# A fused attention and SwiGLU kernel: the halves of the partitions exchanged by token tiles instead of by heads, and one more group scored in 64-key blocks

## The chip, the cores and the metric

The kernel runs on one core of a Trainium2 chip. The core has TensorE (matmul; the profile calls it PE, and its weight loads PEld), VectorE (DVE), ScalarE (ACT), GpSimd (POOL) and SyncE (SP), each with its own queue of instructions worked off in order, and DMA engines that they share. Here POOL issues the loads that convert from float32 to bfloat16, and SP and ACT issue the stores and the transposing DMAs. The metric is the device time of one execution in microseconds (us), the median of several runs.

## The reference

Two parts follow each other: attention over a sliding window of 128 keys plus 4 sink keys at the start of the sequence, and a feed-forward block on its output.

```python
# q, k, v: (4 batches, 8 heads, 768 tokens, 64), float32; n_sink 4, window 128
scores = scale * np.matmul(q, k.transpose(0, 1, 3, 2))
keep = is_sink | ((rel >= 0) & (rel < window))        # rel = query - key
scores = np.where(keep, scores, -1e9)
a = np.exp(scores - max); a = a / (sum(a) + 1e-9)
attn = np.matmul(a, v)
# x: (3072 tokens, 512), the eight heads side by side
g = x @ w_gate                                         # 512 x 1536
out = (silu(g) * (x @ w_val)) @ w_out                  # 1536 x 512
```

## The kernel before

**Groups and tiles.** The 3072 tokens are cut into 12 groups of 256 queries, three for each batch: group g is part c = g % 3 of batch b = g // 3. Attention runs group by group. The feed-forward part runs over eight blocks of 256 or 512 tokens and is cut into units: a `gate` unit is two sets of matmuls of 512 columns in sum (gate, line 506 "pg"; value, line 506 "pv"), with a tanh on ACT (L526) and two products on DVE, `u` (L534) and `ht` (L536, L541 or L545); a `down` unit is the product with `w_out` (L591) and a store.

**The order is written by hand.** The function `weave` goes through a list of units; `slots` says which attention steps are put into which unit, between its gate matmuls and its value matmuls. All engines run their instructions in the order in which they are written. DVE work that is not urgent (masks, normalisations) is collected in a list `later` and put into DVE's queue by `flush`, at the end of a gate unit behind that unit's `u` and `ht`.

**Attention of one group.**
- `load_nat` fetches K and Q (L112, four DMAs from POOL's queue), `load_v` fetches V. Groups 2 and 3 are turned by TensorE (`step_TN`, L265), groups 4 and up by transposing DMAs on SP (`xbar`, L279).
- `step_S` computes scores transposed, keys on the partitions and queries along the columns; ACT takes the exponential out of PSUM (L321, L368) into the tile `e`; DVE multiplies the mask in (L326, L372). It is called twice for a group, for heads 0 to 3 and for heads 4 to 7 (`p2` = 0 and 1), each time for two pairs of heads.
- `step_K` computes the scores of the sink keys. `step_sinks` starts the output of all four PSUM tiles `pos[j, hh]` (j: first or second 128 queries; hh: heads 0 to 3 or 4 to 7) with the sinks' products (L403).
- `step_PV` adds the products with V (L441) for one (j, hh), and normalises (L449, L455, or L452 on ACT). The first `step_PV` of a group calls `step_sinks`.
- `step_X` turns the result for the feed-forward part.

**Two ways of scoring.** Groups with c = 0, and groups 1 and 2, use whole blocks of 128 keys: for a pair of heads and c > 0, three matmuls for each head of 128, 256 and 128 columns on half of the array (64 rows by 128 columns, a head in each half). That gives 512 columns of `e`, a quarter of them in blocks that the window does not reach. PV is two matmuls of 128 keys for each head and each j: 32 for the group.

The groups in the list `QG` (4, 5, 7, 8, 10 and 11) use `step_Sq`: key blocks of 64, on quarters of the array (64 rows by 64 columns). A block of 64 queries meets three blocks of 64 keys, so the four query blocks of a group have twelve such cells. They are laid into six slots of 64 columns with two halves of partitions, 384 columns of `e` for each head. Slots 0 and 1 hold two full halves of keys for j = 0, slots 4 and 5 for j = 1; so PV takes one full matmul of 128 keys for each head and j (16 in the group). Slots 2 and 3 hold the cells that are left, and these take quarter products: 32 matmuls of 64 keys and 64 queries, in `step_sinks` (L414), for all eight heads.

**Which half of the partitions.** A key block goes either to the lower 64 partitions or to the upper 64. In `step_Sq` this is `odd ^ p2`: heads 4 to 7 have the halves exchanged against heads 0 to 3. The mask tile `maskq` therefore has two versions, and the tile of V, `vms[b]` (six slots of 128 partitions for a batch), has a different token layout for heads 0 to 3 and heads 4 to 7; `load_vm` fills it with DMAs of four heads each, ten for c = 1 and six for c = 2 (L127).

**Where things stand in the queues.** POOL's queue begins with loads for groups 0 and 1 and gate weights 0 to 2, then `step_vsb(0)`, K and Q of group 2, gate weights 3, V of group 2 (two DMAs, L147), gate weights 4 and 5, the output weights, K, Q and V of group 3, two memsets, the sinks of the later batches on SP, and `build_maskq` (one memset L332, eight copies L340). The units of group 2 in the first `weave`: its transposes in units 4 (K) and 5 (Q), its scores in units 6 (heads 0 to 3, and `step_K`) and 7 (heads 4 to 7), its PV in unit 8 (heads 0 to 3) and unit 9 (heads 4 to 7), its `step_X` in units 10 and 11. Unit n from 4 to 11 uses gate weights n // 2. Group 3's transposes stand in units 14 and 15, the scores of group 4 in units 19 and 20 and its PV from unit 21.

Of the kernel before, what the change touches and what calls it, by code (L numbers as in the profile page):

```python
# [14 lines left out]
def kernel(  # L15
# [29 lines left out]
    PEX = (0, 1, 2)  # L45
    QG = [g for g in range(4, NG) if g % GC]

# [69 lines left out]
    vms = {}  # L117

    def load_vm(g):

        b, c = divmod(g, GC)
        if b not in vms:
            vms[b] = vpool.tile([P, 6, H, VS], BF16, tag=f"vm{b}", name="vm")
            nc.gpsimd.memset(vms[b][:, :, :, D:D + 1], 1.0)

        def part(t, hs, p0, p1, t0):
            nc.gpsimd.dma_start(  # L127
                vms[b][p0:p1, t - 1, hs, 0:D],
                v[b, hs, t0:t0 + p1 - p0].rearrange("h p d -> p h d"))
        for t in ((1, 2, 3, 4), (4, 5, 6))[c - 1]:  # L130
            if t < 2 * c + 2:
                part(t, slice(0, 4), 0, 64, P * t)
            if t > 3 * c - 2:
                part(t, slice(0, 4), 64, P, P * t - 64)
        for t in ((1, 2, 3, 4), (5, 6))[c - 1]:
            p0, p1 = 64 * (t == 1), P - 64 * (t == 6)
            part(t, slice(4, H), p0, p1, P * t - 64 + p0)

# [32 lines left out]
    mask0 = const.tile([P, 2, 256], BF16)  # L171
    maskq = const.tile([P, 2, 6, 64], BF16)
    diag_h = const.tile([P, 4], BF16)
# [156 lines left out]
    def build_maskq():  # L330

        nc.gpsimd.memset(maskq, 1.0)  # L332
        for hb in range(2):
            for odd in range(2):
                r = slice(64 * (hb ^ odd), 64 * ((hb ^ odd) + 1))
                for m, sl in ((0, (1, 6, 4) if odd else (2, 4, 1)),
                              (1, (2, 4, 1) if odd else (0, 5, 4))):
                    x0_ = P * m + 64 * (hb ^ odd)
                    o = maskq[r, hb, sl[0]:sl[1]:sl[2]]
                    nc.gpsimd.tensor_copy(  # L340
                        out=o, in_=mask[r, 0:1, x0_:x0_ + 64].broadcast_to([64, 2, 64]))

    def step_Sq(g, p2, pps=(0, 1)):

        b, c = divmod(g, GC)
        if g not in e_t:
            e_t[g] = epool.tile([P, H, 512], BF16, tag="e", name="e")
        q0 = c * 256
        runs = (((q0, q0, 192, 0), (q0 + 64, q0 + 64, 192, 192)),
                ((q0 + 128, q0 + 128, 128, 256), (q0 - 64, q0, 128, 0)),  # L350
                ((q0 - 128, q0, 64, 192), (q0 + 192, q0 + 192, 64, 128)))
        pss = {2 * pp + h: bank([P, 384], FP32, "s") for pp in pps for h in range(2)}
        for pp in pps:
            p = 2 * p2 + pp
            for run in runs:
                for odd, (kk, qq, n, col) in enumerate(run):
                    part = slice(64 * (odd ^ p2), 64 * ((odd ^ p2) + 1))
                    for h in range(2):
                        r = slice(h * D, (h + 1) * D)
                        nc.tensor.matmul(  # L360
                            pss[2 * pp + h][part, col:col + n], kTs[b][r, p, kk:kk + 64],
                            qTs[b][r, p, qq:qq + n], start=True, stop=True,
                            skip_group_check=True)
        m = maskq[:, p2].rearrange("q (o a) x -> q o (a x)", o=1)
        for pp in pps:
            h0 = 4 * p2 + 2 * pp
            for h in range(2):
                nc.scalar.activation(  # L368
                    e_t[g][:, h0 + h, 0:384], pss[2 * pp + h], AF.Exp, scale=scale)

            def dve(e=e_t[g][:, h0:h0 + 2, 0:384]):
                nc.vector.tensor_tensor(  # L372
                    e, e, m.broadcast_to([P, 2, 384]), op=ALU.mult)
            later.append(dve)
# [21 lines left out]
    def step_sinks(g):  # L396
# [8 lines left out]
        if g not in QG:  # L405
            return
        for j in range(2):
            col, t = (192, 128)[j], 2 * c + j
            for hq in range(4):
                for odd in range(2):  # L410
                    for hb in range(2):
                        h = 4 * hb + hq
                        r = slice(64 * (odd ^ hb), 64 * ((odd ^ hb) + 1))
                        nc.tensor.matmul(  # L414
                            pos[j, hb][64 * odd:64 * (odd + 1), hq],
                            e_t[g][r, h, col:col + 64],
                            vms[b][r, t + (0 if odd else -2), h, 0:D + 1],
                            start=False, stop=False, skip_group_check=True)

    def step_PV(g, j, hh, norm="v"):  # L420
# [8 lines left out]
        for hq in range(4):  # L429
            h = 4 * hh + hq  # L430
            if g in QG:
                mms.append((po[:, hq], e_t[g][:, h, 256 * j:256 * j + P],
                            vms[b][:, t - 1, h, 0:D + 1]))
                continue
# [288 lines left out]
    load_gate(2)  # L723
    step_vsb(0)
    load_nat(2)
    load_gate(3)
# [9 lines left out]
    load_sinks(vcl, 1, B)  # L736
    build_maskq()

# [109 lines left out]
```

## Time and profile before

| what | value |
|---|---|
| timed runs | 238.07 us median of 3 (237.71 to 238.46) |
| the profiled execution, its own time | 236.61 us |
| its span, first to last instruction | 234.4 us |
| L506 gate and value matmuls, busy | 74.1 and 74.3 us |
| L591 down matmuls, busy | 65.0 us |
| L360 LDWEIGHTS and L314 LDWEIGHTS, number | 288 and 96 |
| L127, V loads in 64-key layout, POOL's queue | 48, 31.4 us |
| L147, other V loads, POOL's queue | 12, 10.7 us |
| L340, copies of `maskq` on POOL | 8, 290 ns each (median) |
| L332, memset of `maskq` on POOL | 1, 737 ns |

The profile is of one execution. Its time is that of the whole execution; the span runs from the first to the last instruction. In a row of a group, "busy" adds the time of all its instructions, and matmuls overlap each other, so starts tell more than busy times of single steps. The granted TensorE clock was 1.000. The DMA engines were busy as follows, in 40 slices of the span (9 is 90% or more):

```profile
DMA  8999999999999979997979999699214100200132
```

### The profile page before, as it was taken

The numbers are of one execution on the slowest core, as the hardware profiler recorded it, in microseconds if no ns is written. First come the engines' busy times: TensorE is split into PE (matmuls) and PEld (weight loads), VectorE is DVE, ScalarE is ACT, GpSimd is POOL, SyncE is SP. The second block draws the span as 40 slices with busy tenths as digits, with TensorE's granted clock in tenths as the row PEclk, the third lists the DMA queues.
The fourth block names the chain that finished last, engine by engine and source line by source line (L and its number), as shares of the span: only waits on it lengthen the run. The fifth ranks groups of instructions, "written<-read, shape, count | busy, mean of one in ns | idle before, by whom it ended". The sixth has DMA issues, their size and how long they took to land.

```text
span 234.4 us, 5418 instructions
## 1 busy us (share of the span) xinstructions
PE 228.7 (98%) x2133; PEld 127.2 (54%) x2133; DVE 154.1 (66%) x327; ACT 108.6 (46%) x230; POOL 98.8 (42%) x150
## 2 busy tenths in 40 slices
PE   8899999999999999999999999999999999999994
PEld 5678545795555654444445444445544444488443
DVE  4898888768550888950888970698960588877000
ACT  4784495367533726422735422755522653333221
POOL 8996865994910619727535295083000000000000
PEclk9999999999999999999999999999999999999999
DMA  8999999999999979997979999699214100200132
GB/s 146 150 187 177 180 200 205 161 140 117 134 154 281 86 106 101 130 196 127 130 115 128 137 120 226 103 97 153 47 22 156 49 3 0 45 3 1 52 127 90
DMA packets 112392, 28.03 MB, mean 120 GB/s; under 512 B 99440, under 2 KB 109424, under 8 KB 112368
## 3 DMA queue, kind: packets, MB, share of 16 engines
q0 software_dynamic: 80288, 14.29, 80.4%
q1 hardware_dynamic: 30672, 11.58, 26.8%
q10 hardware_dynamic: 1408, 1.84, 2.3%
q8 instruction: 16, 0.26, 0.5%
q14 instruction: 8, 0.07, 0.1%
HBM read 29.13 MB, written 6.29 MB: 151 GB/s over the span
## 4 chain that ended last, share of the span: by engine, by line
PE 91%; DMA 2%; POOL 2%; DVE 2%; issue 1%; ACT 1%; POOLq 0%; DVEq 0%; ACTq 0%
PE pd L591 27%; PE pv L506 26%; PE pg L506 26%; PE o L441 4%; DMA rows<-in_q_dram 2%; PE s L360 2%; PE s L314 2%; PE o L414 1%; PE pk L388 1%; PE px L485 1%; PE pn L265 1%; PE o L403 1%; POOL rows L101 1%; POOL x L212 1%; ACT th L526 1%
## 5 line engine op out<-in xcount | busy, mean ns | idle before, releaser
L534 DVE SCALAR_TENSOR_TENSOR u<-th,pg 128x512 bf16<-128x512 f32 x72 | 49.2, 683 | 41.2 <-ACT th L526 41.2
L506 PE MATMUL pv<-xT,wv 128*128 128x512 bf16 (+1 forms) x360 | 74.3, 337 | 0.3 <-DVE xn L455 0.2
L506 PE MATMUL pg<-xT,wg 128*128 128x512 bf16 (+1 forms) x360 | 74.1, 336 | 0.3 <-DVE xT L492 0.2
L526 ACT ACTIVATE th<-pg 128x512 f32<-128x512 f32 x72 | 43.2, 601 | 65.5 <-PE pg L506 65.0
L591 PE MATMUL pd<-wo,ht 128*128 128x512 bf16 (+2 forms) x300 | 65.0, 371 | 0.0
L506 PEld LDWEIGHTS <-wg 128*128 128x128 bf16 x360 | 35.0, 98 | 28.0 <-issue 0.4
L545 DVE TENSOR_TENSOR ht<-u,pv 128x512 bf16<-128x512 bf16 x62 | 42.6, 688 | 9.4 <-PE pv L506 3.9
L591 PEld LDWEIGHTS <-ht 128*128 128x128 bf16 x300 | 27.9, 98 | 30.2 <-issue 0.2
L506 PEld LDWEIGHTS <-wv 128*128 128x128 bf16 x360 | 32.0, 98 | 19.9 <-issue 0.8
L596 ACT ACTIVATE ot<-pd 128x512 f32<-128x512 f32 (+1 forms) x24 | 14.3, 595 | 47.4 <-PE pd L591 47.4
L127 POOL DMA_DIRECT2D vm<-in_v_dram x48 | 31.4, 704 | 2.9 <-DMA nat<-in_k_dram 1.8
L112 POOL DMA_DIRECT2D nat<-in_k_dram x20 | 17.7, 892 | 27.3 <-DMA qT<-nat 25.5
L368 ACT ACTIVATE e<-s 128x384 bf16<-128x384 f32 x48 | 19.6, 502 | 2.8 <-PE s L360 2.8
L455 DVE TENSOR_TENSOR xn<-o,rcp 128x256 bf16<-128x256 f32 x45 | 19.1, 424 | 1.5
L321 ACT ACTIVATE e<-s 128x384 bf16<-128x384 f32 (+1 forms) x40 | 18.1, 550 | 0.3 <-PE s L314 0.2
L112 POOL DMA_DIRECT2D nat<-in_q_dram x20 | 17.7, 899 | 1.3 <-DMA wg<-in_moe_w_gate_dram 1.2
L441 PEld LDWEIGHTS <-e 128*128 128x128 bf16 x256 | 12.3, 98 | 7.4 <-issue 0.2
L372 DVE TENSOR_TENSOR e<-e,maskq 128x768 bf16<-128x768 bf16 x24 | 12.4, 553 | 2.3 <-ACT e L368 2.3
L147 POOL DMA_DIRECT2D va<-in_v_dram x12 | 10.7, 915 | 4.9 <-DMA wo<-in_moe_w_out_dram 2.5
L326 DVE TENSOR_TENSOR e<-e,mask 128x768 bf16<-128x768 bf16 (+1 forms) x20 | 11.3, 605 | 0.4 <-ACT e L321 0.4
L598 DVE TENSOR_SCALAR ot<-pd 128x128 f32<-128x128 f32 x1 | 0.3, 292 | 14.3 <-PE pd L591 14.3
L449 DVE RECIPROCAL rcp<-o 128x4 f32<-128x4 f32 x48 | 8.2, 175 | 2.1 <-PE o L441 1.9
(85 smaller groups left out, 134.6 us busy)
## 6 DMA issues: line engine op xcount, KB each, us to landing
out_dram<-ot SPq DMA_DIRECT2D x17, 256.0 KB
nat<-in_k_dram POOLq DMA_DIRECT2D x20, 128.0 KB, 5.0
nat<-in_q_dram POOLq DMA_DIRECT2D x20, 128.0 KB, 5.5
va<-in_v_dram POOLq DMA_DIRECT2D x12, 128.0 KB, 5.7
wg<-in_moe_w_gate_dram POOLq DMA_DIRECT2D x6, 256.0 KB, 7.2
wv<-in_moe_w_val_dram POOLq DMA_DIRECT2D x6, 256.0 KB, 8.0
wo<-in_moe_w_out_dram POOLq DMA_DIRECT2D x4, 384.0 KB, 11.3
out_dram<-ot ACTq DMA_DIRECT2D x6, 256.0 KB
```

The lines of the kernel that those rows point to most:

```text
L112: nc.gpsimd.dma_start(x[:, i, j].rearrange("p (h d) -> p h d", d=D), src[b, :, t0:t0 + P].rearrange("h p d -> p h d"))
L127: nc.gpsimd.dma_start(vms[b][p0:p1, t - 1, hs, 0:D], v[b, hs, t0:t0 + p1 - p0].rearrange("h p d -> p h d"))
L321: nc.scalar.activation(e_t[g][:, h0 + h, lo:512], pss[2 * pp + h][:, lo:512], AF.Exp, scale=scale)
L368: nc.scalar.activation(e_t[g][:, h0 + h, 0:384], pss[2 * pp + h], AF.Exp, scale=scale)
L441: nc.tensor.matmul(o, l, r, start=(c == 0 and i == 0), stop=(i == len(mms) - 1), skip_group_check=True)
L455: nc.vector.tensor_tensor(xn, po[:, :, 0:D], rcp.broadcast_to([P, 4, D]), op=ALU.mult)
L506: nc.tensor.matmul(ps[:, i * n:(i + 1) * n], ws[fi][:, c, fo * P:(fo + 1) * P], xTs[tb][:, c], start=(c == 0), stop=(c == DMC - 1))
L526: nc.scalar.activation(th, pg, AF.Tanh, scale=0.5)
L534: nc.vector.scalar_tensor_tensor(u, th, 1.0, pg, op0=ALU.add, op1=ALU.mult)
L545: nc.vector.tensor_tensor(hts[tb][:, f:f + 512 // SIZES[tb]].rearrange("p a n -> p (a n)"), u, pv, op=ALU.mult)
L591: nc.tensor.matmul(po, hts[tb][:, f, ts * P:(ts + 1) * P], wos[f // n][:, f % n, lo:hi], start=(f == 0), stop=(f == DFC - 1))
L596: nc.scalar.activation(ot, po, AF.Copy, scale=0.5)
```

## The change

- Group 2 joins the list `QG`, so it is scored by `step_Sq` and its PV uses the quarter products. The list is then 2, 4, 5, 7, 8, 10 and 11.
- Which half of the partitions a key block goes to no longer depends on the head. The exchange depends on the token tile: the key block that stands in the upper half for the first 128 queries' tile and the lower half there are exchanged for the second tile's. `step_Sq` has the same twelve matmuls for a pair of heads in a new order, and in it runs of different lengths stand in the two halves: 192, 192 columns in the upper, 128, 64, 64, 128 in the lower. Before, three runs of 192, 128 and 64 columns were each issued to all four quarters.
- `maskq` has one version instead of two: a memset of half the size, and four copies instead of eight. It is built much earlier, ahead of the K and Q loads of group 2 in POOL's queue.
- `load_vm` loads all eight heads with one DMA: five for c = 1 and three for c = 2. Group 2 has no group before it in `QG`, so it takes five, in place of its two of `load_v`; a memset of the ones column goes from DVE to POOL for it. The tile of batch 0 has four slots, and `lo_slot` says which token tile the first slot is.
- The quarter products in `step_sinks` go head by head, and within a head through j and `odd`; before, they went through j, the head within its four, `odd`, and the two sets of heads. Again four matmuls in a row go to the four quarters.

```diff
-    QG = [g for g in range(4, NG) if g % GC]
+    QG = [g for g in range(2, NG) if g % GC]
...
+    def lo_slot(b):
+        return 1 if b else 3
...
-            vms[b] = vpool.tile([P, 6, H, VS], BF16, tag=f"vm{b}", name="vm")
+            vms[b] = vpool.tile([P, 6 if b else 4, H, VS], BF16, tag=f"vm{b}", name="vm")
             nc.gpsimd.memset(vms[b][:, :, :, D:D + 1], 1.0)
 
-        def part(t, hs, p0, p1, t0):
+        def part(t, p0, p1, t0):
             nc.gpsimd.dma_start(
-                vms[b][p0:p1, t - 1, hs, 0:D],
-                v[b, hs, t0:t0 + p1 - p0].rearrange("h p d -> p h d"))
-        for t in ((1, 2, 3, 4), (4, 5, 6))[c - 1]:
-            if t < 2 * c + 2:
-                part(t, slice(0, 4), 0, 64, P * t)
-            if t > 3 * c - 2:
-                part(t, slice(0, 4), 64, P, P * t - 64)
-        for t in ((1, 2, 3, 4), (5, 6))[c - 1]:
-            p0, p1 = 64 * (t == 1), P - 64 * (t == 6)
-            part(t, slice(4, H), p0, p1, P * t - 64 + p0)
+                vms[b][p0:p1, t - lo_slot(b), :, 0:D],
+                v[b, :, t0:t0 + p1 - p0].rearrange("h p d -> p h d"))
+
+        T = 2 * c
+        if g - 1 not in QG:
+            part(T - 1, 0, 64, P * (T - 1))
+            part(T, 0, P, P * T - 64)
+        part(T + 1, 0, 64, P * (T + 1))
+        part(T + 1, 64, P, P * (T + 1) - 64)
+        if c == GC - 1:
+            part(T + 2, 0, 64, P * (T + 2) - 64)
+        else:
+            part(T + 2, 0, P, P * (T + 2) - 64)
...
-    maskq = const.tile([P, 2, 6, 64], BF16)
+    maskq = const.tile([P, 6, 64], BF16)
...
         nc.gpsimd.memset(maskq, 1.0)
-        for hb in range(2):
-            for odd in range(2):
-                r = slice(64 * (hb ^ odd), 64 * ((hb ^ odd) + 1))
-                for m, sl in ((0, (1, 6, 4) if odd else (2, 4, 1)),
-                              (1, (2, 4, 1) if odd else (0, 5, 4))):
-                    x0_ = P * m + 64 * (hb ^ odd)
-                    o = maskq[r, hb, sl[0]:sl[1]:sl[2]]
-                    nc.gpsimd.tensor_copy(
-                        out=o, in_=mask[r, 0:1, x0_:x0_ + 64].broadcast_to([64, 2, 64]))
+        for up, m, sl in ((0, 0, slice(1, 4, 2)), (0, 1, slice(2, 5, 2)),
+                          (1, 0, slice(2, 6, 3)), (1, 1, slice(0, 4, 3))):
+            r = slice(64 * up, 64 * (up + 1))
+            nc.gpsimd.tensor_copy(
+                out=maskq[r, sl],
+                in_=mask[r, 0:1, P * m + 64 * up:P * m + 64 * up + 64].broadcast_to(
+                    [64, 2, 64]))
...
-        runs = (((q0, q0, 192, 0), (q0 + 64, q0 + 64, 192, 192)),
-                ((q0 + 128, q0 + 128, 128, 256), (q0 - 64, q0, 128, 0)),
-                ((q0 - 128, q0, 64, 192), (q0 + 192, q0 + 192, 64, 128)))
+        runs = ((1, 0, 0, 3, 0), (0, -1, 0, 2, 0), (0, 3, 3, 1, 2),
+                (1, 1, 1, 3, 3), (0, -2, 0, 1, 3), (0, 2, 2, 2, 4))
...
-            for run in runs:
-                for odd, (kk, qq, n, col) in enumerate(run):
-                    part = slice(64 * (odd ^ p2), 64 * ((odd ^ p2) + 1))
-                    for h in range(2):
-                        r = slice(h * D, (h + 1) * D)
-                        nc.tensor.matmul(
-                            pss[2 * pp + h][part, col:col + n], kTs[b][r, p, kk:kk + 64],
-                            qTs[b][r, p, qq:qq + n], start=True, stop=True,
-                            skip_group_check=True)
-        m = maskq[:, p2].rearrange("q (o a) x -> q o (a x)", o=1)
+            for up, kb, qb, n, sl in runs:
+                for h in range(2):
+                    r = slice(h * D, (h + 1) * D)
+                    k0, c0 = q0 + 64 * kb, q0 + 64 * qb
+                    nc.tensor.matmul(
+                        pss[2 * pp + h][64 * up:64 * (up + 1), 64 * sl:64 * (sl + n)],
+                        kTs[b][r, p, k0:k0 + 64], qTs[b][r, p, c0:c0 + 64 * n],
+                        start=True, stop=True, skip_group_check=True)
+        m = maskq.rearrange("q (o a) x -> q o (a x)", o=1)
...
-        for j in range(2):
-            col, t = (192, 128)[j], 2 * c + j
-            for hq in range(4):
+        for h in range(H):
+            for j in range(2):
                 for odd in range(2):
-                    for hb in range(2):
-                        h = 4 * hb + hq
-                        r = slice(64 * (odd ^ hb), 64 * ((odd ^ hb) + 1))
-                        nc.tensor.matmul(
-                            pos[j, hb][64 * odd:64 * (odd + 1), hq],
-                            e_t[g][r, h, col:col + 64],
-                            vms[b][r, t + (0 if odd else -2), h, 0:D + 1],
-                            start=False, stop=False, skip_group_check=True)
+                    t, up = 2 * c + j, j ^ odd
+                    r = slice(64 * up, 64 * (up + 1))
+                    nc.tensor.matmul(
+                        pos[j, h // 4][64 * odd:64 * (odd + 1), h % 4],
+                        e_t[g][r, h, 64 * (3 - j):64 * (4 - j)],
+                        vms[b][r, t - lo_slot(b) + (1 if odd else -1), h, 0:D + 1],
+                        start=False, stop=False, skip_group_check=True)
...
-                            vms[b][:, t - 1, h, 0:D + 1]))
+                            vms[b][:, t - lo_slot(b), h, 0:D + 1]))
...
     step_vsb(0)
+    build_maskq()
     load_nat(2)
...
     load_sinks(vcl, 1, B)
-    build_maskq()
```

## The prediction

> **What bounds the kernel.** I read the page's busy shares first, then the chain that ended last, then stretches of the timeline around group 2, then the DMA issues with their landing times.
>
> ```profile
> PE 228.7 (98%) x2133; PEld 127.2 (54%) x2133; DVE 154.1 (66%) x327; ACT 108.6 (46%) x230; POOL 98.8 (42%) x150
> ...
> PE 91%; DMA 2%; POOL 2%; DVE 2%; issue 1%; ACT 1%; POOLq 0%; DVEq 0%; ACTq 0%
> ```
>
> TensorE is busy for 98% of the span and carries 91% of the chain; behind the first 15 us almost nothing but matmuls is on it. So an edit counts by what it does to TensorE's own time, and by whether it makes TensorE wait. The work on DVE, ACT and POOL counts only through such a wait.
>
> **Group 2's scores.** These are the rows of group 2 as it is now (L314, two calls, the first at 29.41 and the second at 32.02) and of a group that is already scored in 64-key blocks (L360):
>
> ```profile
> 29.48 0.55 PE s L314 x12
> ...
> 60.38 0.46 PE s L360 x24
> ```
> ```profile
> 34.62 0.66 PE L441 MATMUL o<-va,e 128*128 128x65 bf16 x16
> 35.12 0.38 PE L506 MATMUL pv<-xT,wv 128*128 128x512 bf16 x1
> ...
> 83.37 0.45 PE L414 MATMUL o<-vm,e 64*64 64x65 bf16 x32
> 83.75 0.30 PE L441 MATMUL o<-vm,e 128*128 128x65 bf16 x4
> ```
>
> The first pair is from the chain in order of time, the other lines from the timeline; the first column is the start, so differences of starts give what a step costs TensorE. Twelve matmuls of the old form take 0.55 us, twenty-four quarter ones 0.46: two calls give 2 x (0.46 - 0.55) = **-0.18 us**.
>
> **Group 2's PV.** Now: the sinks' four matmuls (L403, from 34.40) 0.22, sixteen L441 in 35.12 - 34.62 = 0.50, sixteen more in 0.48 (36.85 to 37.33); 1.20 in all. After: sinks 0.22, the 32 quarter products 83.75 - 83.37 = 0.38 (it includes the switch back to the whole array, about 0.10), then eight L441 twice at half of 0.48, 0.48; 1.08 in all. That is **-0.12 us**, if nothing has to be waited for.
>
> The extra switch of array form that group 2 gets is in that 0.38. Row first: between the sinks and the next form the starts are 0.22 apart for four concurrent matmuls of 260 columns, some 0.11 of streaming at the 216 ns of a 512-column matmul, so about 0.10 is the switch. The Trainium skill, TensorEngine Tiling (Array Packing), Key Properties, says that changing the tiling form drains TensorE, which speaks against the change; it gives no price, so the sum by it is the row's.
>
> **The wait that it adds.** The quarter products of all eight heads stand in the sinks step, ahead of the first PV of the group. Before, unit 8 needed only heads 0 to 3 there, and heads 4 to 7 one unit later. But the masks of heads 4 to 7 run on DVE only behind unit 7's u and ht:
>
> ```profile
> 31.87 1.28 DVE L326 TENSOR_TENSOR e<-e,mask 128x1024 bf16<-128x1024 bf16 x2
> ...
> 33.85 0.69 DVE L541 TENSOR_TENSOR ht<-u,pv 128x512 bf16<-128x512 bf16 x1
> ...
> 34.46 1.29 DVE L326 TENSOR_TENSOR e<-e,mask 128x1024 bf16<-128x1024 bf16 x2
> ...
> 65.12 0.56 DVE L372 TENSOR_TENSOR e<-e,maskq 128x768 bf16<-128x768 bf16 x1 [0.21 <-ACT e L368]
> ...
> 77.23 1.02 DVE L372 TENSOR_TENSOR e<-e,maskq 128x768 bf16<-128x768 bf16 x2
> ```
>
> After the change DVE runs: masks of heads 0 to 3 from 31.87 - 0.09 = 31.78; two at a pitch of 0.47 (1.02 for two, less 0.55 for one) to 32.72; u (0.78 to the next start, 33.07 to 33.85); ht from 33.50 (0.61 to the next start); masks from 34.11 and 34.58, the last ending at 35.13. Group 4 shows the price of handing over: its last mask ends at 65.12 + 0.56 = 65.68, and its L414, begun at 65.59, take 0.46 to the next form at 66.05, not 0.38. With 0.06 for the semaphore and 0.07 for the eight quarter products of the last two heads they end at 35.26. TensorE reaches them at 34.62 - 0.18 = 34.44 and would be done at 34.44 + 0.28 = 34.72 unhindered. **Wait: +0.54 us.** If DVE gained nothing by the smaller masks, the last would end at 34.46 + 0.60 + 0.55 = 35.61 and the wait be 1.02; if ht came as soon as pv allows (0.05 earlier), 0.49. I take 0.54. Behind the waiting matmul stand all later PE instructions, so nothing hides it; ACT's tanh of unit 8 and DVE merely gain slack.
>
> ACT's exps shrink as well (1.64 for four of 384 columns against 2.06 for four of 512); since ht, not the exp, holds the masks, this is worth nothing here.
>
> **The new order inside the quarters, all seven groups.** The trace has no run of unequal halves. Before, the four quarters get runs of equal length together; now the upper half gets 192, 192 and the lower 128, 64, 64, 128 columns, 384 each as before. Lower bound: 768 columns at 216 ns per 512 are 0.32, with the switch 0.42 instead of 0.46, -0.04 for each of 14 calls, -0.6. Upper bound, if a half must wait for the other: 192 + 192 + 64 + 128 = 576 columns instead of 384, +0.08 for each of 28 pairs of heads, +2.2. For L414 the new order fills each quarter once in four, as the old did: from 32 x 0.03 / 4 = 0.24 instead of 0.28 to half overlap, 0.48; seven groups, -0.3 to +1.4. I take 0 for both, nearest to the L360 and L414 rows: same counts, same lengths in each quarter. By the Trainium skill, TensorEngine Tiling (Array Packing), Key Properties, tiles work independently, by which the sum would also be 0; no run here shows unequal lengths yet. With heads in order, group 4's wait shrinks by some 0.03; left out.
>
> **POOL and the DMAs.** Early on POOL gets, ahead of group 2's K and Q: one memset of half the old 0.74 and four copies of 0.29, about 1.5 us; then a memset of 0.35 and five V loads instead of two (four at the 0.69 of L127, one at the 0.89 of L147, 3.7 instead of 1.78). Queued behind it on POOL are K, Q, gate weights 3, V, gate weights 4 and 5, the output weights and group 3.
>
> ```profile
> 15.04 1.83 POOL L112 DMA_DIRECT2D nat<-in_k_dram  x2
> 16.85 1.77 POOL L112 DMA_DIRECT2D nat<-in_q_dram  x2
> ...
> 20.70 0.89 POOL L147 DMA_DIRECT2D va<-in_v_dram  x1 [0.58 <-DMA wg<-in_moe_w_gate_dram]
> 23.08 0.88 POOL L147 DMA_DIRECT2D va<-in_v_dram  x1 [1.49 <-DMA wv<-in_moe_w_val_dram]
> ```
>
> The DMA engines are busy for 90% or more of every slice there, and the transfers land in order: K, issued at 15.04 and 15.95, lands 8.1 us later, at 23.1 and 24.1, though the shortest load of this shape needs 3.6. Issued 1.5 later, it still queues, so I cost this at nothing: the cover is the queue, and the 2.07 us that POOL waits at 20.70 and 23.08 absorb the lateness. If the cover is gone, K lands at 25.6 against its use at 25.0 (transposes of unit 4): +0.6. POOL's waits end with the landing of the DMA eight issues before (gate weights 2 at 20.4, for the one at 20.70); with more and smaller loads in that list there are still about 0.9 MB under way, over 5 us of queue. V adds 128 KB, at the 157 GB/s of the stretch from 20.5 to 24 0.83 us for everything behind it. Due times: gate weights 4 land at 30.9, now about 31.9, used at 33.3; V at about 30.3, used at 34.4; group 3's first Q at 45.6, now 46.5, used at 47.1. All fit, the last by half a us. The 2.9 us of mask building that leave POOL at 41 to 43.9 let group 4's K and Q keep nearly their times; they are used at 60. SP's transposes of group 4 wait for them and start some 0.6 later; POOL's next load waits for those at 57.8, which is 2.5 ahead of the use.
>
> From group 4 on there are 24 V loads instead of 48; POOL waits more than 25 us for transposes there, so that is worth nothing.
>
> **Sum.** -0.18 - 0.12 + 0.54 = **+0.24 us** against a profiled execution of 236.61 (span 234.4 and 2.2 around it). That execution lies 1.46 below the median of the timed runs, 238.07, which themselves span 237.71 to 238.46; I add the difference to the median: **238.3**. What a measurement here can tell from no change is about 0.3%, 0.7 us.
>
> **Rivals.**
> 1. Slower: *the unequal halves wait for each other* in L360. Place: each pair of heads of seven groups; price up to 0.08 x 28 = 2.2, time up to 240.5; from 17 ns a pair (0.24 + 28 x 0.017 = 0.7) it decides. For it: no row has unequal halves in flight. Against it: the quarters' starts today need no common barrier to explain 0.46.
> 2. Slower: *K of group 2 lands late* because the masks are now built ahead of it: +0.6, 238.9. For it: 0.9 us between landing and use. Against it: a landing time twice the shortest.
> 3. Faster: *no wait and tighter packing.* Without the wait -0.30, 237.8, which is still within the bound; with both lower bounds of the packing (-0.9) 236.9, half of them 237.3. For it: heads in order let the first heads start. Against it: DVE's order puts the masks behind ht.
>
> **How the numbers follow.** Forecast 0.56, its own range 237.7 to 238.9: of this same 0.48, slower 0.06, faster 0.02 for the scatter of the median. Rival 1 0.16, all slower. Rival 2 0.10: slower 0.08, same 0.02. Rival 3 0.18: faster 0.10, same 0.08. Faster 0.12, same 0.58, slower 0.30. The range 237.2 to 239.6 takes in rival 2, half of rival 3 and over half of rival 1.
>
> **What would show it.** Right: L360 in group 2 at 0.46, the L414 of group 2 some 0.9 from first to next form against 0.38 in groups 5 to 10, with the mask of heads 6 and 7 as their releaser; L360 and L414 elsewhere unchanged; no wait ahead of L265 at 25 and 47. Wrong: L360 above 0.48 (rival 1), an idle TensorE before the transposes at 25 (rival 2), L414 of group 2 at 0.4 (rival 3).

## The result, and the profile after

The changed kernel takes **239.13 us** (median of 22 runs, 237.25 to 242.40) against **237.81 us** of the kernel before in the same session (22 runs, 236.75 to 241.03): a ratio of **1.0057**, 95% interval 1.0032 to 1.0082. It is slower, by some 1.3 us. The forecast of 238.3 had the sign and its range holds the time, but it foresaw +0.24, a change too small to be told from none, and gave a slower kernel 0.30. Measured again in another session (the last experiment, e12), the same kernel gave 1.0020 (0.9982 to 1.0057), which can't be told from none. Medians and ranges here and below are of all runs, while the ratios leave out those over 1.5% above the fastest of their kernel, so a ratio need not be the quotient of the medians beside it.

The first lines are from the page of the changed kernel: busy shares, and engines on the chain that ended last. Its span is 236.0 us.

```profile
PE 229.0 (97%) x2173; PEld 127.2 (54%) x2173; DVE 154.5 (65%) x326; ACT 108.2 (46%) x230; POOL 87.1 (37%) x126
...
PE 81%; DMA 7%; POOL 3%; DVE 2%; ACT 2%; issue 2%; SPq 1%; POOLq 0%; DVEq 0%; ACTq 0%
```

TensorE is busy for 0.3 us more in a span 1.6 us longer (profiled executions 237.85 and 236.61). POOL fell from 98.8 to 87.1 us, which is worth nothing. The line to read is the second: DMA rose from 2% of the chain to 7%. Some 3% of this are gate weights at the start, where before it was 2% of query rows; the rest, `xT` with 3% and `qT` with 2%, is new. That transfers are now on the path behind the start is what the forecast did not have.

The stretch of the timeline in which group 2's PV runs, the place of the wait that was forecast (start, duration, engine, line, operation; in brackets the idle time before it and its releaser):

```profile
33.56 0.69 DVE L541 TENSOR_TENSOR ht<-u,pv 128x512 bf16<-128x512 bf16 x1
34.17 1.02 DVE L374 TENSOR_TENSOR e<-e,maskq 128x768 bf16<-128x768 bf16 x2
...
34.52 0.51 PE L414 MATMUL o<-vm,e 64*64 64x65 bf16 x24
...
35.24 0.26 PE L414 MATMUL o<-vm,e 64*64 64x65 bf16 x8 [0.21 <-DVE e L374]
...
35.43 0.42 PE L441 MATMUL o<-vm,e 128*128 128x65 bf16 x8
```

The last masks stand on DVE behind ht and end at 34.17 + 1.02 = 35.19; the eight quarter products of the last two heads wait for them and the next form starts at 35.43. The quarter products hold TensorE from 34.52 to 35.43, 0.91 us, of which 0.38 are theirs.

TensorE further on, in four windows of its timeline: group 3's Q, the feed-forward at 77, group 6's scores, the feed-forward at 148.

```profile
47.19 0.75 PE L271 MATMUL pn<-ident,nat 128*128 128x128 bf16 x8
...
75.94 1.05 PE L506 MATMUL pv<-xT,wv 128*128 128x256 bf16 x8
76.99 1.03 PE L506 MATMUL pg<-xT,wg 128*128 128x256 bf16 x8
...
89.02 0.51 PE L320 MATMUL s<-qT,kT 64*128 64x256 bf16 x8 [0.70 <-DMA qT<-nat]
...
147.92 0.82 PE L506 MATMUL pg<-xT,wg 128*128 128x512 bf16 x3 [0.42 <-DMA xT<-xn]
```

And the kernel before, the matmuls that answer to those at 76.99:

```profile
76.43 1.04 PE L506 MATMUL pg<-xT,wg 128*128 128x256 bf16 x8
```

The pg at 76.99 should have followed the pv at 75.94 after 0.88, as the pair of starts 76.99 and 77.86 does; it follows after 1.05. At 89.02 and 147.92 the bracket names the releaser outright: a transposing DMA.

I matched the two kernels' matmuls one by one and took the difference of their starts. Its steps add up to the difference of the spans:

```
where                                            step, us
start (differs between executions of one kernel)  +0.05
group 2: score calls                              -0.07, -0.07
group 2: PV, first unit / second unit             +0.67 / -0.24
group 2: step_X                                   -0.02             group 2 in all +0.26
group 3's Q late (47)                             +0.14
group 4, heads in order                           -0.09
xT late (77)                                      +0.16
qT late (89)                                      +0.36
xT late (148)                                     +0.58
later score calls, ten steps of 13 ns             +0.13
sum                                               1.60
```

Group 2 itself cost what was forecast. **1.2 of the 1.6 us are waits for transfers**, at places that the forecast did not follow. This is one execution, of 237.85 us; what those nearer to the median of 239.13 waited for was not profiled.

**Where the lateness comes from.** POOL's timeline, first of the kernel before, then after, around the loads of group 5's K and Q and the landing of the feed-forward input that POOL's L624 waits for:

```profile
57.82 1.78 POOL L112 DMA_DIRECT2D nat<-in_k_dram  x2 [3.05 <-DMA qT<-nat]
75.94 0.18 POOL L624 CAST warmed<-xT 1x1 f32<-1x1 bf16 x1 [10.76 <-DMA xT<-xn]
```
```profile
15.97 1.92 POOL L342 COPY maskq<-mask 64x128 bf16<-64x128 bf16 x4
17.84 1.84 POOL L112 DMA_DIRECT2D nat<-in_k_dram  x2
...
59.44 1.75 POOL L112 DMA_DIRECT2D nat<-in_k_dram  x2 [6.84 <-DMA qT<-nat]
76.91 0.18 POOL L624 CAST warmed<-xT 1x1 f32<-1x1 bf16 x1 [11.92 <-DMA xT<-xn]
```

And SyncE's queue of transposing DMAs behind it, before and after:

```profile
62.03 3.31 SPq L279 DMA_TRANSPOSE kT<-nat  x2
65.43 2.58 SPq L480 DMA_TRANSPOSE xT<-xn  x2
68.10 3.81 SPq L279 DMA_TRANSPOSE qT<-nat  x2
72.00 2.56 SPq L480 DMA_TRANSPOSE xT<-xn  x2
```
```profile
62.88 3.97 SPq L285 DMA_TRANSPOSE kT<-nat  x2
66.94 2.53 SPq L480 DMA_TRANSPOSE xT<-xn  x2
69.56 2.69 SPq L285 DMA_TRANSPOSE qT<-nat  x2
72.34 3.02 SPq L480 DMA_TRANSPOSE xT<-xn  x2
```

Read in order, this is one chain. Group 5's K and Q go into the single buffer that group 4's transposes read, so POOL holds their issue until those have ended: 57.82 before, 59.44 after. SyncE issues in order kT of group 5, an xT, qT of group 5, another xT; the last xT is the feed-forward input of the pg at 76.43 (76.99 after). Its landing, as POOL's L624 sees it, moves from 75.94 to 76.91. Before there were 76.43 - 75.94 = 0.5 us of slack. After there is none: the landing is 0.1 us behind the 76.8 at which TensorE could have begun.

### The profile page after: what moved, and what is told of

Its sections match the earlier page's. It is cut to its first block, busy times and chain, and to the rows that moved or that the text cites. A ratio compares the mean times of both kernels' runs of the same rounds, so it can differ in the third digit from the quotient of the medians.

```text
span 236.0 us, 5479 instructions
## 1 busy us (share of the span) xinstructions
PE 229.0 (97%) x2173; PEld 127.2 (54%) x2173; DVE 154.5 (65%) x326; ACT 108.2 (46%) x230; POOL 87.1 (37%) x126
## 4 chain that ended last, share of the span: by engine, by line
PE 81%; DMA 7%; POOL 3%; DVE 2%; ACT 2%; issue 2%; SPq 1%; POOLq 0%; DVEq 0%; ACTq 0%
PE pv L506 25%; PE pg L506 24%; PE pd L591 23%; DMA xT<-xn 3%; PE o L441 3%; DMA wg<-in_moe_w_gate_dram 3%; PE s L362 2%; DMA qT<-nat 2%; POOL va L153 1%; SPq L285 1%; PE s L320 1%; POOL rows L101 1%; PE o L414 1%; DVE e L374 1%; PE pn L271 1%
## 5 line engine op out<-in xcount | busy, mean ns | idle before, releaser
L370 ACT ACTIVATE e<-s 128x384 bf16<-128x384 f32 x56 | 22.9, 502 | 2.8 <-PE s L362 2.8
L130 POOL DMA_DIRECT2D vm<-in_v_dram x29 | 21.5, 778 | 0.6 <-issue 0.4
L374 DVE TENSOR_TENSOR e<-e,maskq 128x768 bf16<-128x768 bf16 x28 | 14.5, 552 | 2.3 <-ACT e L370 2.3
L441 PEld LDWEIGHTS <-e 128*128 128x128 bf16 x240 | 11.8, 98 | 7.3 <-issue 0.2
L327 ACT ACTIVATE e<-s 128x384 bf16<-128x384 f32 (+1 forms) x32 | 14.0, 532 | 0.9 <-PE s L320 0.8
L153 POOL DMA_DIRECT2D va<-in_v_dram x10 | 8.9, 922 | 3.8 <-DMA wo<-in_moe_w_out_dram 3.6
L332 DVE TENSOR_TENSOR e<-e,mask 128x768 bf16<-128x768 bf16 (+1 forms) x16 | 9.3, 623 | 0.4 <-ACT e L327 0.4
```

What stands on the lines that cost most here:

```text
L130: nc.gpsimd.dma_start(vms[b][p0:p1, t - lo_slot(b), :, 0:D], v[b, :, t0:t0 + p1 - p0].rearrange("h p d -> p h d"))
L370: nc.scalar.activation(e_t[g][:, h0 + h, 0:384], pss[2 * pp + h], AF.Exp, scale=scale)
L374: nc.vector.tensor_tensor(e, e, m.broadcast_to([P, 2, 384]), op=ALU.mult)
L441: nc.tensor.matmul(o, l, r, start=(c == 0 and i == 0), stop=(i == len(mms) - 1), skip_group_check=True)
```

## The experiments

Three theories. **A**: group 2's V loads make all later transfers late, and the lateness travels through the K and Q loads and SyncE's queue to xT and qT. **B**: it is the new shape of the later groups' V loads. **C**: only the wait at 35 us is real, the rest is scatter between executions. Each kernel was timed beside the kernel before, e1 to e4, e5 to e8 and e9 to e12 in a session each; "xT(4)" is the landing that L624 reads, "nat(5)" the issue of group 5's K.

**e1: the exchange alone**, group 2 left as it was.

```diff
-    QG = [g for g in range(2, NG) if g % GC]
+    QG = [g for g in range(4, NG) if g % GC]
...
     step_vsb(0)
-    build_maskq()
     load_nat(2)
...
     load_sinks(vcl, 1, B)
+    build_maskq()
```

> The halves exchanged by token tiles for groups 4, 5, 7, 8, 10 and 11 alone; group 2 is scored in whole blocks and the mask is built where it was before. Theory A (group 2's five V loads make the transfers late from 30 us on, and the chain of K and Q loads and transposes carries that to the end): no more waits for transposes than before, 0.0 to +0.3 us against before, of which 0.16 is the unequal runs (12 calls at 0.474 instead of 0.461 us). Theory B (the V loads of eight heads, in a denser burst, hold up the transposes of the later groups): +0.9 to +1.3 us, with the waits at the second half of unit 5 of the block from 74 us and ahead of the block from 147 us still there.

236.41 us (12 runs, 236.21 to 238.15; before 236.72): **0.9972** (0.9944 to 1.0001). POOL's timeline of this kernel:

```profile
57.04 1.75 POOL L112 DMA_DIRECT2D nat<-in_k_dram  x2 [6.14 <-DMA qT<-nat]
73.78 0.18 POOL L624 CAST warmed<-xT 1x1 f32<-1x1 bf16 x1 [11.19 <-DMA xT<-xn]
```

nat(5) goes out 0.8 earlier than before, xT(4) lands 2.2 earlier, and no late transfer stops TensorE behind 45 us; its matmuls end with an offset of +0.05. The later groups' loads are in this kernel as they are in the change, so **B falls**. The price of the unequal halves is in it too. Of the change it leaves out group 2's V loads and the early mask together; the traces tell these apart. In the change, with the mask built ahead, the first V load of group 2 still lands at 28.85 (28.94 before); gate weights 4, behind the five V loads, land at 32.49 (30.85 before). So the lateness comes in at the V loads.

**e2: lateness alone.** The kernel before, with two more loads of 64 KB behind group 2's V, into a tile that nothing reads.

```diff
     load_v(2)
+    vx = vpool.tile([P, 2, H, VS], BF16, tag="vx", name="vx")
+    for j in range(2):
+        nc.gpsimd.dma_start(
+            vx[0:64, j, :, 0:D],
+            v[0, :, 512 + 128 * j:576 + 128 * j].rearrange("h p d -> p h d"))
     load_gate(4)
```

> The kernel before with two further loads of 64 partitions and eight heads (64 KB each) behind group 2's V, into a tile that nothing reads. Theory A: gate weights 4 land 1.3 to 1.7 us later than 30.9, group 4's Q about as much later than 52.0, and the time rises by 0.6 to 1.4 us with no other edit, through waits for transposed tiles after 75 us. Theory B: the lateness is hidden, within 0.3 us of before.

238.46 us (236.92 to 239.57): **1.0043** (1.0011 to 1.0075). TensorE's timeline of it:

```profile
74.54 1.03 PE L506 MATMUL pg<-xT,wg 128*128 128x256 bf16 x8 [0.47 <-DMA xT<-xn]
76.47 0.53 PE L360 MATMUL s<-qT,kT 64*64 64x192 bf16 x24 [0.90 <-DMA qT<-nat]
...
79.20 1.03 PE L506 MATMUL pg<-xT,wg 128*128 128x256 bf16 x8 [0.99 <-DMA xT<-xn]
```

No computation was changed, and in this execution 128 KB of extra loads at 24 us go with 2.4 us of waits 50 us later. That execution took 239.22 us; over the timed runs the loads cost 0.4%, some 1.0 us. nat(5) went out at 60.35, xT(4) landed at 79.12. The core of **A is shown**: more bytes on the V loads' place alone make these waits. Two things are not explained. Some 0.5 us of lateness were there before the extra loads were issued (group 2's K landed at 23.68, in the kernel before at 23.15). And group 4's Q was 0.9 late here (52.75 for 51.86), less than in the change (53.96), yet nat(5) was later than in the change.

**e3: the wait at 35 us alone taken away.** Group 2's quarter products of heads 4 to 7 go into the next unit, ahead of the PV that needs them.

```diff
-        if g not in QG:
-            return
-        for h in range(H):
+        if g in QG and g != 2:
+            step_quarters(g, range(H))
+
+    def step_quarters(g, heads):
+        b, c = divmod(g, GC)
+        for h in heads:
...
             step_sinks(g)
+        if g == 2 and j == 0:
+            step_quarters(g, range(4 * hh, 4 * hh + 4))
```

> The changed kernel, with group 2's quarter products for heads 4 to 7 put off to the unit in which they are next needed. Both theories: the wait of 0.54 us at 35 is gone and two switches of the array's form (0.2 us) come in, so TensorE is 0.35 us earlier at 38 us. Where it ends tells how hard the late transfers bind: -0.35 us against the changed kernel if the later waits follow TensorE, about 0 if they follow the transfers alone.

237.73 us (236.60 to 239.97): 1.0028 (0.9992 to 1.0063). At 40 us TensorE's offset against its start is -0.16 instead of +0.26, a gain of 0.41 where 0.35 was expected. The late transfers stay: xT(4) at 76.55, a step of 0.3 at 147, and one of 0.50 ahead of group 5's scores, which wait for qT:

```profile
75.48 0.54 PE L362 MATMUL s<-qT,kT 64*64 64x192 bf16 x24 [0.42 <-DMA qT<-nat]
```

Theory C would have had the kernel at the time of the one before; the interval allows it. What speaks against C is e2, which has no wait at 35 us and is slower.

**e4: two buffers for the loaded K and Q**, so that group 5's loads need not wait for group 4's transposes (and a pool of one buffer for the last output tiles).

```diff
-    natp = pool("natp", 1)
+    natp = pool("natp", 2)
...
+    olast = pool("olast", 1)
...
-            ot = opool.tile([P, hi - lo], FP32, tag=f"ot{hi - lo}", name="ot")
+            ot = (olast if last else opool).tile([P, hi - lo], FP32, tag=f"ot{hi - lo}", name="ot")
```

> The changed kernel with two buffers for K and Q of a group, so that a load no longer waits for the transposes of the group before (the last output tiles get a pool of their own to make room). Theory A: the lateness of 30 us is no longer carried, the waits after 75 us go, 0.6 to 1.2 us faster than the changed kernel. Theory B: loads and transposes overlap even more, no gain or up to 0.5 us slower.

240.15 us (6 runs, 239.65 to 241.74): **1.0116** (1.0065 to 1.0166). A miss, in the wrong direction. Two waits of TensorE in this kernel (engine and line, releaser: us in total, times, longest):

```profile
PE s L363 <- DMA qT<-nat: 2.0, 1, 2.0
PE s L363 <- DVE u L535: 1.7, 1, 1.7
```

The loads of group 5 now go out at 51.8 and run beside group 4's transposes on DMA engines that are already full. The transposes end later, and group 4's scores wait 2.0 us for qT, until 62.6. The second wait is ahead of group 8's scores at 129; what ended it is not clear, since the page names a DVE instruction. In the profiled execution (241.74 us) the granted clock also fell to 0.50 from 63.2 to 66.6 us, right behind the first wait, where TensorE lost another 1.5 us. Three of the six runs had a clock of 1.000 and took 240.1 to 240.2, so the clock is not what makes this kernel slow. The buffer was not what made the transfers late, it only kept the next loads from standing in front of the transposes.

**e5: one V load less in group 2.** The change, but group 2's quarter products take those 64 keys from the tile that an earlier group loaded.

```diff
         if g - 1 not in QG:
-            part(T - 1, 0, 64, P * (T - 1))
+            if g != 2:
+                part(T - 1, 0, 64, P * (T - 1))
...
+                    vx = (vas[1][r, 1, h, 0:D + 1] if g == 2 and j == odd == 0 else
+                          vms[b][r, t - lo_slot(b) + (1 if odd else -1), h, 0:D + 1])
```

> The changed kernel with one of group 2's five V loads left out: its lower half of the slot before the group holds the same tokens as group 1's V tile, so the eight quarter products that need it read that tile. Theory A, in the form that the first runs left of it (late K and Q of group 5 hold SP's queue, and the transposes of the feed-forward input stand behind them): the loads behind V land 0.4 to 0.8 us earlier, the wait of 0.54 at 35 us stays, the waits after 75 us shrink; 0.2 to 0.6 us faster than the changed kernel. Theory C (the wait at 35 us alone makes the change slower, the rest is scatter of the transfers between executions): within 0.2 us of the changed kernel.

237.42 us (236.58 to 241.22; before 237.01): 1.0007 (0.9973 to 1.0042). In its profile nat(5) goes out at 59.56 and xT(4) lands at 76.98, no earlier than in the change, with waits of 0.09 for group 5's qT at 75 and of 0.54 at 89. The loads in between were earlier than in the change (group 4's Q 53.55 for 53.96). So the profile shows no gain from 64 KB less; the median is better than the change's, by less than the intervals can tell.

**e6: V ahead of K and Q** for groups 5 and 7 to 11.

```diff
     def NV(g):
-        return L(A(load_nat, g), A(load_v, g))
+        fs = [A(load_nat, g), A(load_v, g)]
+        return L(*(fs if g == 4 else fs[::-1]))
```

> The changed kernel with V loaded ahead of K and Q in groups 5 and 7 to 11, so that V's transfers fall into POOL's wait for the transposes before and no longer beside the transposes of the feed-forward input. Theory A: the input of the block from 74 us is there up to 1 us earlier than 76.9, the waits after 75 us shrink, 0.3 to 0.9 us faster than the changed kernel; if V delays the transposes of group 4 instead, TensorE waits ahead of group 4's scores at 61 and the time rises by up to 1 us. Theory C: within 0.2 us.

240.39 us (238.28 to 244.44): **1.0115** (1.0079 to 1.0151). A miss again. nat(5) goes out at 61.18, xT(4) lands at 78.94:

```profile
76.46 0.54 PE L362 MATMUL s<-qT,kT 64*64 64x192 bf16 x24 [0.86 <-DMA qT<-nat]
79.02 1.03 PE L506 MATMUL pg<-xT,wg 128*128 128x256 bf16 x8 [0.81 <-DMA xT<-xn]
```

Issued in what I took for idle time, V's loads stand in front of group 4's transposes and delay the very event that nat(5) waits for.

**e7: the edits of e3 and e5 together.**

> The changed kernel with both mends: group 2's quarter products for heads 4 to 7 put off by a unit, and the V load left out. Theory A: 0.6 to 1.1 us faster than the changed kernel, from 0.0 to +0.5 us against before. Theory C: 0.4 us faster than the changed kernel, all of it from the split.

237.74 us (236.37 to 240.80): 1.0013 (0.9980 to 1.0046). Its profiled execution ends with an offset of +0.25, of which +0.34 were there at the start, and has no wait for a transfer (xT(4) at 76.33); this execution took 236.42 us, and the median, 1.3 above, suggests that others have them. The two together don't beat either alone.

**e8: the exchange alone (e1) with e6's edit.**

> The exchange by token tiles alone, group 2 in whole blocks, with V loaded ahead of K and Q in groups 5 and 7 to 11. Exchange alone had no wait for transposes left, so by theory A this gives 0.0 to -0.3 us against it, and is 0.3 to 0.6 us faster than before; by theory C the same.

236.75 us (236.24 to 237.81): 0.9983 (0.9953 to 1.0013). xT(4) lands at 76.25, where e1 had 73.78: the edit costs the same 2 to 2.5 us of lateness as in e6, and here the slack swallows it. So what costs 1.9 us of waiting in one kernel costs nothing measurable in the other.

**e9: K, Q and V of group 3 and K, Q of group 4 loaded ahead of the output weights.**

```diff
-    for i in range(4):
-        load_out(i)
     load_nat(3)
     load_v(3)
+    load_nat(4)
+    for i in range(4):
+        load_out(i)
...
-        (11, [NV(4), lambda: nc.gpsimd.tensor_copy(out=vcl[64:128], in_=vcl[0:64])]),
+        (11, [A(load_v, 4), lambda: nc.gpsimd.tensor_copy(out=vcl[64:128], in_=vcl[0:64])]),
```

> The changed kernel with K, Q and V of group 3 and K and Q of group 4 loaded ahead of the output weights, which are not used before 54 us; nothing else is moved. Theory A (late K and Q): group 4's K and Q land some 6 us earlier, the loads and transposes of the later groups have slack again, the input of the block from 74 us is there before 74.5, and no wait for a transfer is left behind 60 us; what stays is group 2's own cost of 0.3 us, so +0.0 to +0.5 us against before and 0.6 to 1.2 us faster than the changed kernel beside it. Theory C (scatter, and the wait at 35 us alone): within 0.2 us of the changed kernel.

240.57 us (6 runs, 238.86 to 243.93): **1.0106** (1.0032 to 1.0179). The third miss of the same kind, and the one that says most. SyncE's queue and POOL of this kernel:

```profile
47.51 2.68 SPq L285 DMA_TRANSPOSE kT<-nat  x2
```
```profile
60.73 1.75 POOL L112 DMA_DIRECT2D nat<-in_k_dram  x2 [9.59 <-DMA qT<-nat]
79.05 0.18 POOL L624 CAST warmed<-xT 1x1 f32<-1x1 bf16 x1 [12.76 <-DMA xT<-xn]
```

Group 4's Q landed 8.8 us earlier than in the change (45.17 against 53.96) and its transposes were issued 3.5 us earlier (47.51 against 51.06). Yet POOL, which waits for their end, issues nat(5) 1.3 us *later*; with the same order e10 issues it 1.5 later than e7, and e11 1.6 later than e1. What nat(5) follows is the end of the loads issued ahead of it: in every kernel of the table below the last of them, a V load, lands 0.3 to 2.0 us before nat(5) goes out (at 57.94 in the change, 59.98 here), however early the transposes were issued. Why the same loads end 2 us later in this order the runs don't show.

**e10 and e11: e9's load order in e7 and in e1.**

> Split quarter products, the V load left out, and the early K and Q together. Theory A: -0.3 to +0.2 us against before, and narrow between executions; theory C: like the run with the first two mends, +0.1 to +0.5 us.

> The exchange alone, group 2 in whole blocks, with the early K and Q. It had no wait for transfers left in its profile, so both theories expect no more than 0.2 us against the exchange alone: -0.2 to -0.7 us against before.

e10: 239.38 us (237.72 to 243.36; before 236.96), **1.0049** (1.0012 to 1.0087), nat(5) 60.52, xT(4) 79.19, a step of 3.0. e11: 236.42 us (236.20 to 238.13), 0.9977 (0.9948 to 1.0006), nat(5) 58.65, xT(4) 76.09, no wait. The order does no harm that shows where there is slack, and where there is none it goes with 3.0 us of waits in e10's profile.

**e12: the change itself once more**, beside those.

> The changed kernel as it is, beside the others on one chip: +0.8 to +1.9 us against before, by the first measurement; TensorE's wait at 35 us again 0.4 to 0.6 us, and one to three waits for transposes behind 70 us of 0.1 to 1 us each, not the same as in the first profile in size.

237.45 us (236.85 to 242.64): 1.0020 (0.9982 to 1.0057). Its profile, first TensorE, then POOL:

```profile
76.96 1.04 PE L506 MATMUL pg<-xT,wg 128*128 128x256 bf16 x8
```
```profile
76.87 0.18 POOL L624 CAST warmed<-xT 1x1 f32<-1x1 bf16 x1 [12.05 <-DMA xT<-xn]
```

In this execution xT(4) lands 0.09 ahead of its use and no transfer stops TensorE; group 2 costs +0.25 as in the first profile. TensorE itself came to this place 0.14 us later than in the first profile, as it had lost 0.3 us more at the start, which helped. The change sits on the edge: its transfers are just in time in one execution and cost 1.2 us of waits in another.

All of it in one table, in order of the landing:

```
kernel   nat(5) issued   xT(4) landed   step of TensorE at 74 to 78 us   ratio
e1           57.04          73.78            0                           0.9972
before       57.82          75.94            0                           1
e11          58.65          76.09            0                           0.9977
e8           59.11          76.25            0                           0.9983
e7           59.07          76.33            0                           1.0013
e3           59.49          76.55            0.50                        1.0028
e12          59.26          76.87            0                           1.0020
change       59.44          76.91            0.16                        1.0057
e5           59.56          76.98            0.09                        1.0007
e6           61.18          78.94            1.9                         1.0115
e9           60.73          79.05            1.8                         1.0106
e2           60.35          79.12            2.8                         1.0043
e10          60.52          79.19            3.0                         1.0049
```

The step adds up the wait of group 5's scores for qT and that of the matmuls behind them for xT; the 0.50 of e3 and the 0.09 of e5 are waits for qT alone. Up to 76.33 no kernel waits. Between 76.5 and 77.0 it depends on the execution; from 78.9 on all wait 1.8 us or more, and all four have an interval above 1, as the change has in its first measurement. (e4 has another order of loads and is left out.) Within the lower group the ratios don't follow the landing closely, since later waits of the same kind, at 90 and 148, come on top. No version is faster than the kernel before by more than its interval; e1 comes nearest.

## Why the forecast was right in sign and short in size

- **Group 2's scores**, -0.18: measured -0.07 and -0.07. Right.
- **Group 2's PV and the wait**, -0.12 + 0.54 = +0.42: measured +0.67 - 0.24 = +0.43. The first unit holds 0.38 of quarter products less the 0.24 of eight L441 that go, so its wait is 0.67 - 0.14 = 0.53, with 0.54 taken. e3 takes this wait away and gains 0.41.
- **Unequal halves**, taken as 0: starts of successive score calls show 0.474 us against 0.461 for a call, 13 ns, at most 0.18 over 14 calls. Rival 1's price of 2.2 is out, and its turning point of 17 ns a pair isn't reached (13 ns for a call of two pairs). The Trainium skill, TensorEngine Tiling (Array Packing), Key Properties, has tiles work independently; these 13 ns agree to within 3% of a call.
- **Group 2's K late** (rival 2): issued 2.8 us later (17.84 against 15.04), it landed at 23.13, against 23.15. The queue covered it, as the forecast argued. Rival 3 is out with the wait shown.
- **The term that was mis-sized** is the one costed at nothing: "All fit, the last by half a us", and the "2.5 ahead of the use" of POOL's wait at 57.8. It failed in two ways. First the lateness: "0.83 us for everything behind it" was 1.6 (gate weights 4, 32.49 for 30.85), 1.8 (group 3's K, 45.59 for 43.79) and 2.1 (group 4's Q, 53.96 for 51.86) in the first profile, and 1.2 at both ends in e12's (32.06 and 53.04). V's five loads of group 2 are 384 KB and land over 3.3 us (28.08 to 31.40), 118 GB/s, where the forecast used 157; that they are smaller need not be the reason, since the two 64 KB loads of e2 landed within 0.8 us. Group 3's first Q, given half a us to spare, landed at 47.49 instead of 45.62, just too late for its transposes, and cost 0.14; the forecast's sign "no wait ahead of L265 at 25 and 47" fails at 47. Second, and larger: the chain was followed to the first use of each load and no further. POOL's wait at 57.8 was compared with the use of group 4's own K and Q at 60; what it holds back, nat(5), and through SyncE's queue xT(4), was not followed. The rows for it were in the trace of before: landing 75.94, use 76.43, 0.5 of slack against a lateness of at least the 0.83 that the forecast itself had. Taken at nothing, this term measured 1.2 us of waits in the first profile.
- **Fewer V loads in the later groups**, "worth nothing": e1 points to a small gain (xT(4) 2.2 earlier, ratio 0.9972), which its interval doesn't settle.

So the parts of the forecast that concern group 2 came out, and its total came out small by the one term. That its range still holds 239.13 is luck: the upper end was there for rivals 1 and 2, and neither came.

What stays open: how large the change's loss is. Its two measurements, 1.0057 and 1.0020, have overlapping intervals, and so do e3, e5 and e7, so whether mending parts of it helps was not settled. Nor was it shown how the lateness of group 4's loads becomes that of nat(5): 0.9 us became 2.5 in e2, and 2.1 became 1.6 in the change. A version with less DMA work ahead of 57 us, which the last runs point to, was not tried.

## What to carry to other kernels

When an edit adds bytes to a DMA queue that is already full, follow the lateness through every later load and every in-order queue to the tightest use, not to the first, and compare it with the smallest slack on the way. While the engines are full, moving loads forward in the order need not make transposes on the same engines end sooner: here three such edits (e4, e6, e9) made the kernel 1% slower. A kernel whose transfers are just in time shows its loss in some executions only, so one profile without waits is no proof that there are none.

## What the hardware showed that was not expected

- Beside a full queue of loads, issuing transposing DMAs earlier did not bring their end forward: in e9 they were issued 3.5 us earlier, and the next load, which waits for their end, went out 1.3 us later. A second buffer (e4) cost 1.2%.
- In e4's profiled execution the granted TensorE clock fell to 0.50 for 3.4 us right behind a wait of 2.0 us. In e10 the same wait, 2.3 us at 79 us, left it at 1.00, so the wait alone doesn't set it off.
- POOL's mask copies took 1.92 us for four at 16 us, 0.48 each, and 1.09 for four, 0.27 each, at 41 us in e1. At 16 us DVE ran mask products with two inputs in SBUF beside them, which took 3.11 us for four there, 0.78 each, against 2.49 for the same four at 14.96 in the kernel before, 0.62 each, where no mask copies ran. At 41 us DVE ran u and ht, each with one input from PSUM. The Trainium skill, SBUF — State Buffer, Who interferes with whom, says that a VectorE instruction with two SBUF inputs contends with a GpSimd instruction that reads SBUF; the two rows agree with it, though no run here separates it from other causes.
- A load issued 2.8 us later landed at the same time, 23.13 for 23.15; the load ahead of it in the queue landed at 22.27 and 22.31.
